# Half of chunk 1's first matrix product by two groups of seven half-size products

## The chip, the core and the metric

One NeuronCore of a Trainium2 chip runs the kernel. Its engines work side by side, each on its own list of instructions, and wait for each other by semaphores: TensorE (PE, with its weight loads shown apart as PEld) multiplies matrices into PSUM, VectorE (DVE) and GpSimd (POOL) do elementwise work, ScalarE (ACT) evaluates functions (Gelu, exp) and copies, and SyncE (SP) issues most transfers. The metric is the device time of one execution in microseconds (us); lower is better.

## The reference

A linear attention, whose result is the input of a two-layer network with an exact Gelu:

```python
# q, k, v: (8 batches, 8 heads, 576 positions, 64)
q_s = softmax(q, axis=-1)          # over the 64 channels
k_s = softmax(k, axis=2)           # over the 576 positions
kv  = einsum('bhsd,bhse->bhde', k_s, v)
x   = einsum('bhsd,bhde->bhse', q_s, kv)
x   = x.transpose(0, 2, 1, 3).reshape(8 * 576, 512)
h   = x @ w_in                     # w_in: 512 x 2048
g   = 0.5 * h * (1 + erf(h / sqrt(2)))
out = g @ w_out                    # w_out: 2048 x 512
```

Inputs and output are float32; the kernel multiplies in bfloat16.

## The kernel before

The 4608 tokens are worked off in nine chunks of 512: chunk c = 0 to 7 holds the first 512 positions of batch c, chunk 8 the last 64 positions of all batches. Every chunk goes through the same stages: exponentials of q and k (ScalarE, `exp_q`, `exp_k`), sums and reciprocals of q (VectorE, `q_sums`) and the multiplication by them (`q_scale`, VectorE or GpSimd), kv = k_s^T v (`kv_mm`, line 231), q transposed (`xbar_step`, a transposing DMA, from batch 2 on), x (`x_mm`), h, Gelu into the tile `g`, and y = g @ w_out (`y_phase`).

The order of the work is written out by hand: an engine carries out its instructions in the order in which the code issues them. Batches run ahead of chunks: while y of chunk c is computed, kv and x of chunk c + 1 and the softmax of batch c + 2 are prepared. `y_phase` takes a dictionary of such insertions, called at numbered points (`after(0)` to `after(10)`).

h of one chunk has 16 tiles of 128 rows. Plainly (chunks 0 and 1), each tile is 4 products of 512 columns (`h_mm`, line 393) and one Gelu (`h_gelu`, line 399). From chunk 2 on `h_waves` computes h by seven half-size products instead of eight (a scheme of the Strassen kind): for each group q of four tiles, 7 products of 4 matmuls with 256 columns each (line 513). Products 1, 2 and 4 take blocks of w_in as they are (`wi_bf`), products 5, 6, 7 and 3 take sums s1 to s4 of blocks (`quad_s`, made once by `quad_weights`: group 0, 1 from `quad_weights(0)`, group 2, 3 from `quad_weights(1)`). Products 4 to 7 multiply sums t1 to t4 of blocks of x (`quad_t`, `x_sums`). The four PSUM results are combined: `seed` copies product 1 (bank A) into bank C, `p5_copy` copies product 5 (bank B) to `r` in SBUF, `e_sum` adds A (after product 6) and r into B, `r_sum` adds A (after product 7) and r into r. Products 7 and 4 accumulate into A and so come after the sums that read it. Gelu is then taken of C, r, A and B.

y too is computed by seven products from chunk 1 on (`y_operands`): its operands are sums of blocks of g (`s5`, `s12`, and differences in place, all by `s_parts`, on VectorE) and mixed blocks of w_out (`mix_wo`: 1 and 6 into `w16`, 7 into `w7`, 3 and 4 in place). From chunk 3 on the product of the quarter blocks in y is itself done by seven products of a smaller size (class `Two`, weights by GpSimd, `y3.weights`).

Around chunk 1, in the order of the code: GpSimd casts three of the four head pairs of v(1) (`cast_v`, line 196); x of chunk 1 comes in two halves with the first tiles of h between; four tiles of h (`t1s`) are finished; VectorE makes the last mixed blocks (lines 1168 to 1171); `h_pairs` computes the other twelve tiles in pairs p = 2 to 7 and, after a pair or two, VectorE makes the sums s5 and s12 and the differences (`s_ops`). ScalarE casts v(2) after the pairs p = 3 to 6. VectorE makes s1, s2 and s3 of `quad_weights(1)` beside it, s4 at the start of `y_phase(1)`. Then come `exp_q(2)` and `exp_k(2)` on ScalarE and the products of y: 4 (into `bd`), 5 (`be`), 1 (`ba`), 2 (again into `bd`), then kv of batch 2, then 3, 6 and 7, x of chunk 2, kv of batch 3 and h of chunk 2. Between product 4 and product 2 the bank `bd` is copied to `f`.

In chunk 2, `h_waves` calls `q_late` in the middle: GpSimd multiplies q(3) as a whole, `xbar_step(3)` transposes it, and GpSimd makes the last three weight sums of `Two`.

Of the kernel before, what the change touches and what calls it, by code (L numbers as in the profile page):

```python
# [16 lines left out]
def kernel(  # L17
# [142 lines left out]

    def exp_q(b, parts=1):

        e = attn_sb.tile([128, J, H, D], BF16, tag="eq")
        st[b]["eq"] = e
# [13 lines left out]
        for i, u in sets:  # L178
            nc.scalar.activation(out=dst[:, i], in_=src[:, u], func=AF.Exp)  # L179
# [98 lines left out]

    def q_scale_parts(b):

        for j in range(J):
            for i in (0, 4):
                e = st[b]["eq"][:, j, i:i + 4, :]
                nc.gpsimd.tensor_tensor(  # L284
                    out=e, in0=e, op=ALU.mult,
                    in1=st[b]["recq"][:, j, i:i + 4].unsqueeze(2).to_broadcast([128, 4, D]),
                )
# [113 lines left out]
    def s_parts(c, p0, n, which):  # L401
# [14 lines left out]
        for i, half in ((3, lo), (4, hi)):  # L416
            if i in which:
                tt(out=s12[:, a, half], in0=g[:, a, half], in1=g[:, b, hi], op=ALU.add)  # L418
        if 2 in which:
            tt(out=g[:, a, hi], in0=g[:, a, hi], in1=g[:, a, lo], op=ALU.subtract)  # L420
            tt(out=g[:, b, lo], in0=g[:, b, lo], in1=g[:, b, hi], op=ALU.subtract)  # L421

# [24 lines left out]

    def quad_weights(w):

# [3 lines left out]
        a21, a22 = wi_bf[:, 0:2, dn], wi_bf[:, 2:4, dn]  # L453
        s1, s2, s3, s4 = (q[:, i] for i in range(4))
        return [
            lambda: tt(s1, a21, a22), lambda: tt(s2, s1, a11, ALU.subtract),
            lambda: tt(s3, a11, a21, ALU.subtract), lambda: tt(s4, a12, s2, ALU.subtract),
        ]
# [19 lines left out]
    def h_waves(c, mid, sums=None):  # L478

        h_begin(c)
        g, xT = st[c]["g"], st[c]["xT"]
# [8 lines left out]
        if mid:  # L492
            bank_of.update(B=("kv0", "kv1") * 2, C=("x1", "x2") * 2)
        held = {}

        def take(kind, q):
            held[kind, q] = bank(roles[bank_of[kind][q]], "q" + kind.lower(), (128, 2, HT))

# [39 lines left out]

        vcopy, scopy = nc.vector.tensor_copy, nc.scalar.copy
        mm(1, 0, 1)  # L540
        seed(0)
        if mid:
# [12 lines left out]
            e_sum(1)  # L555
            mid()
            mm(2, 2, 3)
            gelu("C", 2, 3)
            mm(7, 0, 1)
            r_sum(0)  # L560
            r_sum(1)
            mm(3, 0, 1)
            gelu("B", 0, 1)
# [130 lines left out]
    class Two:  # L694
# [11 lines left out]
        def weights(self, part):  # L706
# [9 lines left out]
            tt(o[2], b21, b11, ALU.subtract, eng=eng)  # L716
            tt(o[3], b11, b12, eng=eng)
            tt(o[4], b21, b22, eng=eng)
            w = self.w[:, 4]
# [58 lines left out]
    def y_phase(c, ins, p3=None):  # L778
# [30 lines left out]
        if p3:  # L809
            p3.mm(c, bx, (4, 5, 1), True)  # L810
            p3.snap(bx)
        mm(4, bd, True)
        if c > 1:
# [8 lines left out]
        else:  # L822
            nc.vector.tensor_copy(out=f, in_=bd)
        after(0)
# [169 lines left out]

    def mix_wo(m, a):

# [11 lines left out]
        }[m]  # L1008
        nc.vector.tensor_tensor(out=o, in0=i0, in1=i1, op=op)

# [89 lines left out]
    w16 = wst.tile([128, 2, HK, HN], BF16, tag="w0", name="w16")  # L1100
    sums = quad_weights(1)
    mix_wo(6, 0)
# [20 lines left out]
    mix_wo(3, 0)  # L1123
    mix_wo(4, 0)
    cast_wo(3, wo[3], 2, 1)
    cast_wo(3, wo[3], 3, 1)
# [155 lines left out]
```

## Time and profile before

| | |
|---|---|
| median of 3 runs | 255.77 us (255.7 to 255.9) |
| the profiled execution | 255.87 us, span 253.9 us |
| mean granted TensorE clock | 0.997 |
| VectorE: two-input bf16 sum, 128x1024 (L409) | 684 ns each, x14 |
| GpSimd: multiplication of q, 128x256 (L284) | 653 ns each, x40 |
| GpSimd: cast of v, 128x576 (L196) | 711 ns each, x25 |
| ScalarE: exponential of k, 128x2304 (L184) | 2120 ns each, x6 |

The span runs from the first instruction to the last; the execution's own time is 1.97 us longer. Durations are means over all instructions of that form. An instruction may begin a little before the one ahead of it has ended, so that start-to-start times in the timeline are often 0.1 us below the durations.

### The profile page before, as it was taken

The numbers are of one execution on the slowest core, as the hardware profiler recorded it, in microseconds if no ns is written. First come the engines' busy times: TensorE is split into PE (matmuls) and PEld (weight loads), VectorE is DVE, ScalarE is ACT, GpSimd is POOL, SyncE is SP. The second block draws the span as 40 slices with busy tenths as digits, with TensorE's granted clock in tenths as the row PEclk, the third lists the DMA queues.
The fourth block names the chain that finished last, engine by engine and source line by source line (L and its number), as shares of the span: only waits on it lengthen the run. The fifth ranks groups of instructions, "written<-read, shape, count | busy, mean of one in ns | idle before, by whom it ended". The sixth has DMA issues, their size and how long they took to land.

```text
span 253.9 us, 6825 instructions
## 1 busy us (share of the span) xinstructions
PE 247.9 (98%) x2738; PEld 196.1 (77%) x2738; DVE 219.1 (86%) x395; ACT 190.4 (75%) x326; POOL 102.8 (40%) x177
## 2 busy tenths in 40 slices
PE   7999999999999999999999999999999999999994
PEld 3444444448888888898889988998889889988883
DVE  1878898788987997998999899989999999868972
ACT  4785978699977996889688968896887788248711
POOL 1530023000978459106950596059603960560000
PEclk9999999999999999999999999999999999999998
DMA  7999999995329999890569255810520061004033
GB/s 239 397 367 420 405 406 400 401 407 206 61 64 288 375 265 377 246 340 5 188 196 310 98 188 177 204 36 3 165 87 3 1 193 57 3 4 165 0 84 84
DMA packets 43168, 50.24 MB, mean 198 GB/s; under 512 B 20225, under 2 KB 30465, under 8 KB 42881
## 3 DMA queue, kind: packets, MB, share of 16 engines
q1 hardware_dynamic: 42416, 49.13, 57.8%
q10 hardware_dynamic: 720, 0.69, 1.0%
q8 instruction: 21, 0.34, 0.6%
q14 instruction: 11, 0.08, 0.1%
HBM read 36.70 MB, written 9.44 MB: 182 GB/s over the span
## 4 chain that ended last, share of the span: by engine, by line
PE 81%; DMA 16%; DVE 1%; SPq 0%; issue 0%
PE qa L513 19%; PE ya L799 10%; PE qb L513 10%; PE yd L799 10%; DMA f<-in_q_dram 7%; PE ye L799 6%; PE ps L393 6%; PE yb L799 5%; PE qc L513 5%; DMA w<-in_moe_w_out_dram 3%; DMA w<-in_moe_w_in_dram 3%; PE yx L753 3%; DMA f<-in_v_dram 2%; PE kv L231 2%; PE ps L359 1%; PE ya L882 1%
## 5 line engine op out<-in xcount | busy, mean ns | idle before, releaser
L513 PEld LDWEIGHTS <-quad_s 128*128 128x128 bf16 x448 | 43.8, 98 | 5.1
L799 PEld LDWEIGHTS <-g 128*128 128x128 bf16 x368 | 35.2, 98 | 4.8 <-issue 0.4
L513 PEld LDWEIGHTS <-wi_bf 128*128 128x128 bf16 x336 | 32.8, 98 | 3.9
L799 PEld LDWEIGHTS <-s 128*128 128x128 bf16 x336 | 32.7, 98 | 3.7
L513 PE MATMUL qa<-quad_t,quad_s 128*128 128x256 bf16 x224 | 29.2, 273 | 0.0
L275 POOL TENSOR_TENSOR e<-e,recq 128x1024 bf16<-128x1024 bf16 (+1 forms) x4 | 9.3, 2330 | 47.8 <-DVE recq L270 41.0
L393 PE MATMUL ps<-xT,wi_bf 128*128 128x512 bf16 x128 | 28.1, 379 | 0.2 <-DVE kvc L244 0.2
L444 POOL TENSOR_TENSOR y_sb<-y_sb 128x128 f32<-128x128 f32 x56 | 26.0, 498 | 2.8 <-issue 2.8
L269 DVE TENSOR_REDUCE qsum<-e 128x16 f32<-128x1024 bf16 (+1 forms) x12 | 20.9, 1746 | 6.8 <-ACT e L179 6.5
L284 POOL TENSOR_TENSOR e<-e,recq 128x256 bf16<-128x256 bf16 x40 | 24.7, 653 | 1.8 <-DVE recq L270 1.2
L393 PEld LDWEIGHTS <-wi_bf 128*128 128x128 bf16 x128 | 12.4, 98 | 15.3 <-issue 0.7
L521 ACT COPY qc<-qa 128x512 f32<-128x512 f32 x26 | 13.9, 577 | 11.4 <-PE qa L513 5.3
L399 ACT ACTIVATE g<-ps 128x512 bf16<-128x512 f32 x32 | 17.6, 602 | 6.1 <-PE ps L393 5.8
L179 ACT ACTIVATE e<-f 128x512 bf16<-128x512 f32 (+1 forms) x42 | 20.5, 556 | 2.1 <-DMA f<-in_q_dram 1.9
L537 ACT ACTIVATE g<-r 128x512 bf16<-128x512 f32 x28 | 17.3, 631 | 6.3 <-DVE r L444 6.3
L444 DVE TENSOR_TENSOR qb<-qa,r 128x512 f32<-128x512 f32 x28 | 18.1, 691 | 4.1 <-PE qa L513 1.6
L537 ACT ACTIVATE g<-qc 128x512 bf16<-128x512 f32 x28 | 15.2, 594 | 7.4 <-PE qc L513 7.4
L418 DVE TENSOR_TENSOR s<-g 128x1024 bf16<-128x1024 bf16 x28 | 19.8, 726 | 0.0
L196 POOL CAST v_aug<-f 128x576 bf16<-128x576 f32 x25 | 17.0, 711 | 4.4 <-DMA f<-in_v_dram 4.3
L444 DVE TENSOR_TENSOR r<-qa,r 128x512 f32<-128x512 f32 x28 | 17.9, 680 | 0.7 <-PE qa L513 0.7
L184 ACT ACTIVATE ek<-f 128x2304 bf16<-128x2304 f32 (+1 forms) x10 | 17.2, 1734 | 1.2 <-DMA f<-in_k_dram 1.2
L1213 POOL CAST scr<-g 128x1 f32<-128x1 bf16 x4 | 0.7, 187 | 42.3 <-DVE g L421 42.3
(117 smaller groups left out, 550.2 us busy)
## 6 DMA issues: line engine op xcount, KB each, us to landing
out_dram<-y_sb SPq DMA_DIRECT2D x16, 512.0 KB, 3.9
f<-in_k_dram SPq DMA_DIRECT2D x6, 1152.0 KB, 9.5
f<-in_v_dram SPq DMA_DIRECT2D x6, 1152.0 KB, 10.5
f<-in_q_dram SPq DMA_DIRECT2D x6, 1024.0 KB, 7.6
w<-in_moe_w_in_dram SPq DMA_DIRECT2D x6, 512.0 KB, 8.9
f<-in_v_dram SPq DMA_DIRECT2D x8, 288.0 KB, 6.5
f<-in_q_dram SPq DMA_DIRECT2D x4, 512.0 KB, 9.0
w<-in_moe_w_out_dram SPq DMA_DIRECT2D x2, 1024.0 KB, 11.4
```

What stands on the lines that cost most here:

```text
L179: nc.scalar.activation(out=dst[:, i], in_=src[:, u], func=AF.Exp)
L184: nc.scalar.activation(out=ek[b % 2][:, i:i + n], in_=st[b]["kf"][:, i:i + n].rearrange("p x (n d) -> p x n d", n=NS), func=AF.Exp,)
L196: eng.tensor_copy(out=o, in_=i)
L269: nc.vector.reduce_sum(out=qsum, in_=st[b]["eq"][:, :, i * w:(i + 1) * w, :], axis=AX.X)
L284: nc.gpsimd.tensor_tensor(out=e, in0=e, op=ALU.mult, in1=st[b]["recq"][:, j, i:i + 4].unsqueeze(2).to_broadcast([128, 4, D]),)
L393: nc.tensor.matmul(ps, wi_bf[:, dm, t * 128:(t + 1) * 128], st[c]["xT"][:, dm, :], start=(dm == 0), stop=(dm == NDM - 1),)
L399: nc.scalar.activation(out=st[c]["g"][:, t, :], in_=ps, func=AF.Gelu)
L418: tt(out=s12[:, a, half], in0=g[:, a, half], in1=g[:, b, hi], op=ALU.add)
L444: eng.tensor_tensor(out=out, in0=in0, in1=in1, op=op)
L513: nc.tensor.matmul(held[kind, q][:, u], w, mov[m][:, k], start=(m in (1, 5) and u == 0 and k == 0), stop=(k == 1), skip_group_check=True,)
L537: nc.scalar.activation(out=g[:, t:t + 2, half], in_=held[kind, q], func=AF.Gelu)
L799: nc.tensor.matmul(ps[:, j * HN:(j + 1) * HN], act[m][:, k, j * 128:(j + 1) * 128], wgt[m][:, k, :], start=(first and k == 0 and j == 0), ...
```

## The change

Of chunk 1's h, the tiles of the second half of each block (groups q = 2, 3; tiles 4 to 7 and 12 to 15) are computed by the seven products; the tiles of p = 0 to 3 stay plain. So `h_waves` gets a branch for chunk 1, with its own banks, and `h_pairs` isn't called any more. `quad_weights(1)` must be ready earlier: s1 is made by VectorE ahead of the last casts of w_out, s2 to s4 by GpSimd in four pieces of 128x256 each, and the mixed blocks 1 and 3 of the second half likewise; they stand behind the casts of v(1) in GpSimd's order, and ahead of all four casts of v(2), which move from ScalarE to GpSimd. VectorE gets the four sums of x of chunk 1, the sums of A and r, and the copies of r.

In `y_phase(1)`, ScalarE makes the copy f of `bd` (VectorE before), between the two halves of `exp_q(2)`; `exp_k(2)` follows. The multiplication of the first half of q(2) is done by GpSimd in four pieces, and the sums and multiplication of q(3) are split in halves, the second half in the middle of chunk 2's h, behind the weight sums of `Two`, which are in pieces of half the size.

```diff
-    def exp_q(b, parts=1):
+    def exp_q(b, parts=1, part=None):
...
-            for h in (0, 4):
+            for h in (0, 4) if part is None else (4 * part,):
...
-    def q_scale_parts(b):
+    def q_scale_parts(b, half=None):
...
-            for i in (0, 4):
+            for i in (0, 4) if half is None else (4 * half,):
...
     def quad_weights(w, parts=()):
...
+        def block(i, out, in0, in1, op=ALU.add):
+            if i not in parts:
+                tt(out, in0, in1, op)
+                return
+            for k in range(2):
+                for n in (slice(0, 256), slice(256, 512)):
+                    tt(out[:, k, n], in0[:, k, n], in1[:, k, n], op, eng=nc.gpsimd)
...
     def h_waves(c, mid, sums=None):
...
+        first_banks = {"A": (5, 6), "B": (1, 7), "C": (3, 4)}
+
+        def plain(p):
+            for i, t in ((2, p + HK), (0, p)):
+                ps = bank(i)
+                h_mm(c, ps, t, range(NDM))
+                h_gelu(c, ps, t)
...
+        if c == 1:
+            plain(2)
+            for q in (2, 3):
+                mm(5, q)
+                mm(1, q)
+            seed(2)
+            seed(3)
+            p5_copy(2, vcopy)
+            p5_copy(3, vcopy)
+            mix_wo(4, 1)
+            plain(3)
+            mm(6, 2, 3)
+            e_sum(2)
+            e_sum(3)
+            mm(2, 2, 3)
+            gelu("C", 2, 3)
+            s_parts(c, 2, 2, (0,))
+            mm(7, 2, 3)
+            r_sum(2)
+            r_sum(3)
+            gelu("r", 2, 3)
+            mm(3, 2, 3)
+            mm(4, 2, 3)
+            gelu("A", 2, 3)
+            gelu("B", 2, 3)
+            s_parts(c, 2, 2, (1,))
+            s_parts(c, 4, 4, (0,))
+            s_parts(c, 4, 4, (3,))
+            s_parts(c, 4, 4, (4,))
+            s_parts(c, 2, 2, (2,))
+            s_parts(c, 4, 4, (5,))
+            return
...
     def y_phase(c, ins, p3=None):
...
+        if c == 1:
+            exp_q(2, parts=2, part=0)
         mm(4, bd, True)
...
-            nc.vector.tensor_copy(out=f, in_=bd)
+            nc.scalar.copy(out=f, in_=bd)
+            exp_q(2, parts=2, part=1)
+            exp_k(2)
...
-    def mix_wo(m, a):
+    def mix_wo(m, a, parts=False):
...
+        if parts:
+            for i in range(4):
+                nc.gpsimd.tensor_tensor(out=o[:, i], in0=i0[:, i], in1=i1[:, i], op=op)
...
-    sums = quad_weights(1)
+    sums = quad_weights(1, parts=(2, 3, 4))
...
     mix_wo(4, 0)
+    sums[0]()
...
-    mix_wo(7, 1)
-    mix_wo(4, 1)
-    mix_wo(1, 1)
-    mix_wo(3, 1)
+    for fn in sums[1:]:
+        fn()
+    for m in (1, 3):
+        mix_wo(m, 1, parts=True)
+    cast_v_all(2)
...
-    h1 = {p + 3: [lambda p=p: cast_v(2, p, nc.scalar)] for p in range(HP)}
-    h1[1] = [sums[0]]
-    h1[3] += sums[1:3]
-    h_pairs(1, h1, done=t1s, turn=Banks(2, 0, 5, 6))
-
-
-    exp_q(2, parts=2)
-    exp_k(2)
+    x_sums(1, (1, 2, 3, 4))
+    mix_wo(7, 1)
+    s_ops(1, 0, 2)
+    h_waves(1, None)
...
     y_phase(1, {
-        0: [sums[3]],
-        7: [lambda: norm_q(2, 0, 2)],
-        1: [lambda: norm_q(2, 1, 2, nc.vector)],
+        7: [lambda: q_sums(2, 0, 2), lambda: q_scale_parts(2, 0)],
+        1: [lambda: norm_q(2, 1, 2, nc.vector), lambda: s_parts(1, 4, 4, (6,))],
...
-        3: [lambda: kv_step(2), lambda: exp_k(3), lambda: q_sums(3)],
+        3: [lambda: kv_step(2), lambda: exp_k(3), lambda: q_sums(3, 0, 2)],
...
-        q_scale(3, nc.gpsimd)
+        q_scale_parts(3, 0)
+
+    def q_later():
+        y3.weights(1)
+        q_sums(3, 1, 2)
+        q_scale_parts(3, 1)
         xbar_step(3)
-        y3.weights(1)
...
-        h_waves(c, q_late if c == 2 else None, p3 and p3.sums)
+        h_waves(c, (q_late, q_later) if c == 2 else None, p3 and p3.sums)
```

(`s_parts` numbers 5 and 6 are the two halves of its number 2. In `h_waves`, `mid[0]` stands where `mid` stood, `mid[1]` after the r sums of groups 0 and 1.)

More of the change, by code (lines that the diff above doesn't have):

```diff
@@ L159, in load_qrest @@
             )
-    def exp_q(b, parts=1):
-        e = attn_sb.tile([128, J, H, D], BF16, tag="eq")
-        st[b]["eq"] = e
+    def exp_q(b, parts=1, part=None):
+        if part != 1:
+            st[b]["eq"] = attn_sb.tile([128, J, H, D], BF16, tag="eq", name="e")
+        e = st[b]["eq"]
         dst = e.rearrange("p j h d -> p h j d")
@@ L277, in q_scale @@
         )
-    def q_scale_parts(b):
+    def q_scale_parts(b, half=None):
+        r = st[b]["recq"]
         for j in range(J):
-            for i in (0, 4):
+            for i in (0, 4) if half is None else (4 * half,):
                 e = st[b]["eq"][:, j, i:i + 4, :]
+                i = i if half is None else 0
                 nc.gpsimd.tensor_tensor(
                     out=e, in0=e, op=ALU.mult,
-                    in1=st[b]["recq"][:, j, i:i + 4].unsqueeze(2).to_broadcast([128, 4, D]),
+                    in1=r[:, j, i:i + 4].unsqueeze(2).to_broadcast([128, 4, D]),
                 )
@@ L418, in s_parts @@
                 tt(out=s12[:, a, half], in0=g[:, a, half], in1=g[:, b, hi], op=ALU.add)
-        if 2 in which:
+        if 2 in which or 5 in which:
             tt(out=g[:, a, hi], in0=g[:, a, hi], in1=g[:, a, lo], op=ALU.subtract)
+        if 2 in which or 6 in which:
             tt(out=g[:, b, lo], in0=g[:, b, lo], in1=g[:, b, hi], op=ALU.subtract)
@@ L446, with quad_weights @@
     quad = {"s": {}}
-    def quad_weights(w):
+    def quad_weights(w, parts=()):
         q = quad["s"][w] = wst.tile([128, 4, 2, 512], BF16, tag=("w4", "w1")[w], name="quad_s")
@@ L478, in h_waves @@
     def h_waves(c, mid, sums=None):
-        h_begin(c)
+        if c > 1:
+            h_begin(c)
         g, xT = st[c]["g"], st[c]["xT"]
@@ L494, in h_waves @@
         held = {}
+        first_banks = {"A": (5, 6), "B": (1, 7), "C": (3, 4)}
[4 more added lines that the diff above has]
+                h_gelu(c, ps, t)
         def take(kind, q):
-            held[kind, q] = bank(roles[bank_of[kind][q]], "q" + kind.lower(), (128, 2, HT))
+            i = first_banks[kind][q - 2] if c == 1 else roles[bank_of[kind][q]]
+            held[kind, q] = bank(i, "q" + kind.lower(), (128, 2, HT))
         def mm(m, *qs):
@@ L555, in h_waves @@
             e_sum(1)
-            mid()
+            mid[0]()
             mm(2, 2, 3)
@@ L561, in h_waves @@
             r_sum(1)
+            mid[1]()
             mm(3, 0, 1)
@@ L715, in weights @@
                 return
-            tt(o[2], b21, b11, ALU.subtract, eng=eng)
-            tt(o[3], b11, b12, eng=eng)
-            tt(o[4], b21, b22, eng=eng)
+            for a in range(2):
+                tt(o[2][:, a], b21[:, a], b11[:, a], ALU.subtract, eng=eng)
+                tt(o[3][:, a], b11[:, a], b12[:, a], eng=eng)
+                tt(o[4][:, a], b21[:, a], b22[:, a], eng=eng)
             w = self.w[:, 4]
@@ L1008, in mix_wo @@
         }[m]
-        nc.vector.tensor_tensor(out=o, in0=i0, in1=i1, op=op)
+        if parts:
+            for i in range(4):
+                nc.gpsimd.tensor_tensor(out=o[:, i], in0=i0[:, i], in1=i1[:, i], op=op)
+        else:
+            nc.vector.tensor_tensor(out=o, in0=i0, in1=i1, op=op)
     def warm(n, z):
```

4 lines of the change are left out of this document (2 added, 2 removed).

## The prediction

> **What bounds the kernel now.** I read the page's busy table first, then the chain of waits, then ScalarE's and VectorE's timelines in chunk 1 (40 to 75 us).
>
> ```profile
> span 253.9 us, 6825 instructions
> PE 247.9 (98%) x2738; PEld 196.1 (77%) x2738; DVE 219.1 (86%) x395; ACT 190.4 (75%) x326; POOL 102.8 (40%) x177
> ```
>
> TensorE (PE) is busy 98% of the span. VectorE (DVE) follows at 86%, so what is laid on it has little room.
>
> ```profile
> 45.48 13.06 PE ps L393 x60
> 58.54 1.75 PE yd L799 x16
> 60.28 1.75 PE ye L799 x16
> 62.03 1.75 PE ya L799 x16
> 63.78 1.75 PE yd L799 x16
> 65.52 0.76 PE kv L231 x72
> ```
>
> The chain (start, duration, what) is TensorE without a hole from 44.12 to 250.34 us. So fewer columns on TensorE shorten the kernel one for one, and any wait put into TensorE lengthens it likewise. One 512-column product of h takes 13.06/60 = 0.218 us; a 256-column one takes 0.109 (1.75/16).
>
> ```profile
> 57.90 1.27 ACT L399 ACTIVATE g<-ps 128x512 bf16<-128x512 f32 x2
> 59.19 1.28 ACT L179 ACT_TABLE_LOAD   x1
> 60.48 2.38 ACT L179 ACTIVATE e<-f 128x512 bf16<-128x512 f32 x6
> 62.76 2.11 ACT L184 ACTIVATE ek<-f 128x2304 bf16<-128x2304 f32 x1
> 64.78 2.17 ACT L179 ACTIVATE e<-f 128x512 bf16<-128x512 f32 x4
> ```
>
> ScalarE's timeline (start, duration) between chunk 1's last Gelu and kv of batch 2: the exponentials of k end at 62.76 + 2.11 = 64.87, and TensorE comes to kv at 65.52. The slack is 0.65 us.
>
> ```profile
> 75.07 0.42 DVE L444 TENSOR_TENSOR quad_t<-xT 128x512 bf16<-128x512 bf16 x1
> ...
> 200.29 0.78 DVE L444 TENSOR_TENSOR quad_t<-xT 128x512 bf16<-128x512 bf16 x1
> 200.75 0.79 POOL L284 TENSOR_TENSOR e<-e,recq 128x256 bf16<-128x256 bf16 x1
> 201.17 0.65 DVE L444 TENSOR_TENSOR quad_t<-xT,quad_t 128x512 bf16<-128x512 bf16 x1
> 201.50 0.79 POOL L284 TENSOR_TENSOR e<-e,recq 128x256 bf16<-128x256 bf16 x1
> ```
>
> The same VectorE operation, first with GpSimd (POOL) idle, then with GpSimd multiplying pieces of 128x256. Alone it takes 0.42 us. Beside the pieces it takes 0.78 and 0.65, and the pieces take 0.79 where a piece with no such neighbour takes 0.61 (start 121.06). The two take turns: the second operation ends at 201.82, 0.42 after 201.40, and 201.40 is 0.14 before the end of the piece begun at 200.75. VectorE's sums that read PSUM beside the same pieces keep their 0.68, so only operations with two SBUF inputs wait.
>
> **The change, part by part.** Times are in the coordinates of the profiled execution.
>
> *TensorE.* The tiles of p = 4 to 7, 32 matmuls of 512 columns, become 2 x 28 of 256: 32 x 0.218 = 6.97 against 56 x 0.109 = 6.12, that is -0.85 us. Without waits, h ends at T = 57.69 instead of 58.54, and kv(2) is reached at T + 4 x 1.746 = 64.67.
>
> *ScalarE.* It loses the four casts of v(2) and gains two seeds (0.58 each) and the copy of yd to f (0.46 of start-to-start time, as 66.86 to 67.32). Its last eight Gelus now hang on VectorE: in chunk 2 the last of them ends 3.90 after the first r sum starts (83.16 to 87.06). That sum could start after product 7's first half, 55.51, and behind VectorE's e sums and one s5 sum, 55.55. So the Gelus end at 59.45 at best. Behind that, in the order of the changed program: table load, half of exp_q, f copy, other half, exp_k, 3.57 (59.19 to 62.76) + 0.48 + 2.11 later. exp_k(2) ends at 65.62, 0.75 later than now, while TensorE arrives 0.85 earlier. So even with nothing else wrong kv(2) starts near 65.65 instead of 65.52: **the saving is eaten by a wait of 0.98, net +0.1**. Queued behind kv on TensorE is all that follows.
>
> *GpSimd's new pieces.* Three block sums are 12 pieces of 128x256, two mixed blocks 8 more, behind the casts of v(1), which end at 42.38. Their own form isn't in the trace; the 512-wide weight sums have 1.11 start to start (81.79 to 82.90), so 0.56 for 256, as L284's 0.57. Without neighbours they run to 53.7 and the casts of v(2) to 56.2 (0.62 each); s4 is needed at 55.9, s2 at 53.3, w16 at 61, v(2) at 65. These edits cost GpSimd nothing on the path; with that cover gone it is the last rival.
>
> *What the pieces do to VectorE.* The added x sums and quadrant sums go on VectorE. From 46.17 it has four x sums, mix 7, the four s operations of p = 0, 1, two r copies from PSUM, mix 4, and then the e sum, which TensorE's product 7 waits for. Start-to-start times in the trace:
>
> ```profile
> 46.17 0.68 DVE L1009 TENSOR_TENSOR w<-wo_bf 128x1024 bf16<-128x1024 bf16 x1
> ...
> 49.39 0.43 DVE L409 TENSOR_TENSOR s<-g 128x512 bf16<-128x512 bf16 x1 [0.61 <-ACT g L399]
> ...
> 84.36 0.93 DVE L418 TENSOR_TENSOR s<-g 128x1024 bf16<-128x1024 bf16 x1
> 87.75 0.68 DVE L409 TENSOR_TENSOR s<-g 128x1024 bf16<-128x1024 bf16 x1
> ```
>
> Alone: 4 x 0.33 + 0.60 brings it to 48.1; the s operations wait for Gelu until 49.39 and take 0.34 + 0.72 + 0.34 + 0.34; copies 1.20; mix 0.60. It would be free at 52.9, before the e sum's input (53.81). But ten of these have two SBUF inputs, and GpSimd's pieces run through all of it. With a turn of 0.42 per operation: t1 starts at 46.22, t2 to t4 and mix 7 at 46.97, 47.72, 48.47, 49.22; the s operations at 50.24, 51.00, 52.14, 52.90; copies 53.24 to 54.44; mix 4 waits to 54.82; the e sums run from 55.42 to 56.62. An s5 sum with a turn against a cast comes between, and the first r sum starts near 57.2 instead of 55.55: **+1.65**. Bounds of a turn: 0 (the sum at 97.62 takes its 0.42, between two pieces) and 0.47 (a piece from 200.18 holds 200.29 back to 200.65). I take 0.42, since back to back each side always finds the other waiting. With 0, the net stays +0.1; with 0.2 it is +0.25 (the gate at 49.39 and the slack before the e sum absorb nearly all).
>
> The Trainium skill speaks against this change: its page "SBUF — State Buffer", section "Who interferes with whom", says that a VectorE operation with two SBUF inputs and a GpSimd one that reads SBUF exclude each other, and that whichever issues second is blocked until the first has finished. The trace agrees on the exclusion (the 0.78 and 0.65 above), but its turns end 0.14 before the piece does; what the rule would make of the time, read strictly, is rival 4.
>
> *Sum at kv(2).* Gelus end at 57.2 + 3.90 = 61.10, exp_k at 67.28, kv starts at 67.3: **+1.8**. TensorE itself, held 0.95 at product 7, is there at 65.9 and waits 1.4. Past it, chunk 1 holds: xbar(2) issues near 68.8 and landing takes 3.7 (median of its issues), before x at 73.4; VectorE takes half of q_sums(3) later and is free at 72.8, before ya ends at 73.4.
>
> *Chunk 2.* q_sums(3)'s second half (1.42) fits VectorE's idle 1.46 before 81.57. GpSimd's multiplication of q(3) is split around the weights: 4 pieces to 79.4, six weight pieces 3.4, the negation 1.5, and then four new pieces from 84.3, where VectorE starts s sums. Four turns less the 0.26 already paid at 84.36 move the s5 sum from 87.75 to 89.2, its end to 89.85. TensorE's ye starts at 88.80 and reaches that half 4 x 0.109 later, at 89.24: **+0.6** (0 without turns, 0.8 at 0.47 each). xbar(3) issues some 7 us later than now, near 87.5 against 80.75; x(3) starts at 95.79, so 3.7 for landing is covered; if not, up to 1 us.
>
> *Sum.* 255.87 (this execution's own time; its span is 253.9, 1.97 lies around it) + 1.8 + 0.6 = 258.3; the median 255.77 is 0.1 lower, so **258.2**.
>
> **Rivals.**
> 1. *The pieces hardly hold VectorE back* (turns up to 0.2). For: the sum at 97.62 slips in free, with pieces on both sides. Against: 123.40, 149.04, 174.64 and 200.29 all wait 0.36 or more. Then only ScalarE's delay is left, +0.1 to +0.25: 255.9 to 256.0, not slower.
> 2. *The saving arrives*: the exponentials of k(2) are ready when TensorE is. Place: kv(2); price -0.85, 254.9. It decides at 64.67, and a wait there under 0.34 would still be over 0.2% faster. For: TensorE is otherwise full, and ScalarE loses 2.6 us of casts. Against: from T on ScalarE needs 1.76 for Gelus and 6.18 behind, against TensorE's 6.98.
> 3. *GpSimd becomes the bound*: if every piece waits for a 1024-wide operation (0.6 + 0.47), 20 pieces and four casts end at 42.3 + 21.4 + 4.9 = 68.6, and kv(2) waits for v instead, +1.3 on the forecast: 259.5. Against: half the turns are 0.33 wide, and PSUM operations leave it alone.
> 4. *A turn costs a whole piece*, 0.57 start to start and not 0.42: ten turns add 1.5 to the forecast, 259.7. For: where a piece is itself held back it takes 0.79. Against: 200.29 is let in at 200.65, 0.14 before the piece's end. This is the page's rule by the letter.
>
> **How the numbers follow.** Forecast 0.72 (its own range 256.8 to 259.4: the first term 1.0 to 2.5, the second 0 to 1.1), rival 1 0.14, rival 2 0.06, rival 3 0.04, rival 4 0.04. The likeliest is 258.2. A measurement of this kernel tells 0.2% (0.5 us) from no change; forecast, rival 3 and rival 4 are slower, 0.80, rival 1 same, rival 2 faster. The range, 256.0 to 259.8, takes in rivals 3 and 4 and the edge of rival 1; rival 2 and most of rival 1 are left out.
>
> **What would show it.** Right: chunk 1's x sums near 0.75 apart and GpSimd's sum pieces near 0.8 each between 46 and 53 us; the first r sum of chunk 1 near 57; TensorE idle near 1 us before product 7 and 1.4 before kv(2), released by ScalarE's ek; a short wait at ye of chunk 2 for s. Wrong: x sums 0.33 to 0.4 apart; no wait of TensorE at kv(2); or the wait there released by v_aug. The forecast falls if the last Gelu of chunk 1 ends before 60 us.

## The result, and the profile after

| | before | after |
|---|---|---|
| median, us (lowest to highest of 4 runs) | 255.74 (255.49 to 255.9) | 258.74 (258.61 to 259.58) |
| ratio, 95% interval | | 1.0125 [1.0102, 1.0149] |
| the profiled execution, us (its span) | 255.87 (253.9) | 259.58 (257.8) |

The kernel is slower by 3.0 us (2.6 to 3.8 by the interval); 2.4 was forecast. The profiled execution of the changed kernel is the longest of its four: the spans of the others are 256.8 to 257.0.

The busy table of the changed kernel, and TensorE's waits from 44 us to the end (what waits, for which result, us in total, times, the longest):

```profile
span 257.8 us, 6918 instructions
PE 247.8 (96%) x2762; PEld 198.4 (77%) x2762; DVE 228.4 (89%) x394; ACT 190.0 (74%) x325; POOL 125.8 (49%) x214
```

```profile
PE qa L534 <- DVE qb L448: 1.5, 1, 1.5
PE kv L232 <- ACT ek L185: 1.2, 1, 1.2
PE ye L854 <- DVE s L412: 0.5, 1, 0.5
```

TensorE's busy time is hardly less (247.8 us against 247.9; the ends of matmuls are modelled there and some records are missing, so the saving doesn't show in this sum), and it has three new waits: product 7 for the sums of A and r, kv of batch 2 for the exponentials of k, product 5 of chunk 2's y for the sums s5. These are the three places that the prediction named. The chain of waits of the changed kernel (start, us, what) now leaves TensorE and runs through VectorE and ScalarE:

```profile
46.51 0.97 DVE quad_t L448
47.56 2.33 DVE quad_t L448 x3
49.89 1.07 DVE w L1072
...
54.47 0.69 DVE r L546 x2
56.19 0.74 DVE qb L448 x2
58.23 0.69 DVE r L448
58.94 1.28 ACT g L558 x3
...
62.13 1.28 ACT L180
66.28 2.02 ACT ek L185
68.35 0.83 PE kv L232 x72
92.24 0.61 DVE s L412
92.90 1.48 PE ye L854 x12
```

VectorE is the chain from the first sum of x to the first r sum, ScalarE from there to kv, and a sum s5 ends up on it once more in chunk 2. What stretches VectorE stands in GpSimd's timeline (start, duration, what):

```profile
47.14 3.28 POOL L448 TENSOR_TENSOR quad_s<-wi_bf,quad_s 128x256 bf16<-128x256 bf16 x4
50.38 3.81 POOL L1070 TENSOR_TENSOR w<-wo_bf 128x256 bf16<-128x256 bf16 x4
54.15 3.27 POOL L1070 TENSOR_TENSOR wo_bf<-wo_bf 128x256 bf16<-128x256 bf16 x4
57.37 2.69 POOL L197 CAST v_aug<-f 128x576 bf16<-128x576 f32 x4
```

Pieces of 128x256 take 0.8 to 0.95 us each here.

Where the 3.9 us of this execution are is read from the starts of the same work in TensorE's timeline (by this view kv(2) starts at 65.45 before; the chain of waits, with which the prediction worked, has 65.52):

| us | h of chunk 1 | y of chunk 1 | kv(2) | x(2) | h of chunk 2 | y of chunk 2 | x(3) | last product of chunk 2's y (`ya`) |
|---|---|---|---|---|---|---|---|---|
| before | 44.12 | 58.37 | 65.45 | 71.56 | 72.81 | 85.14 | 95.72 | 96.96 |
| after | 44.46 | 59.99 | 68.35 | 74.45 | 75.70 | 88.26 | 99.55 | 100.80 |
| difference | +0.34 | +1.62 | +2.90 | +2.89 | +2.89 | +3.12 | +3.83 | +3.84 |

(The last column is what the expectations below call chunk 3's last product: the 16 matmuls into `ya` behind kv(3), product 7 of chunk 2's y.) So +2.90 has come about by kv(2), 0.23 in h of chunk 2, 0.71 in its y, and nothing to speak of behind it.

### The profile page after: what moved, and what is told of

It is laid out like the page before. It is cut to its first block, busy times and chain, and to the rows that moved or that the text cites. A ratio compares the mean times of both kernels' runs of the same rounds, so it can differ in the third digit from the quotient of the medians.

```text
span 257.8 us, 6918 instructions
## 1 busy us (share of the span) xinstructions
PE 247.8 (96%) x2762; PEld 198.4 (77%) x2762; DVE 228.4 (89%) x394; ACT 190.0 (74%) x325; POOL 125.8 (49%) x214
## 3 DMA queue, kind: packets, MB, share of 16 engines
q1 hardware_dynamic: 42416, 49.13, 57.4%
## 4 chain that ended last, share of the span: by engine, by line
PE 76%; DVE 11%; ACT 4%; DMA 4%; issue 2%; POOL 1%; SPq 0%; DVEq 0%; ACTq 0%
PE qa L534 19%; PE qb L534 9%; PE ya L854 9%; PE yd L854 7%; PE ps L396 6%; PE qc L534 5%; PE yb L854 5%; PE ye L854 5%; PE yx L808 3%; DMA f<-in_v_dram 2%; PE kv L232 2%; PE ps L362 2%; DMA f<-in_q_dram 2%; PE ya L941 1%; PE yd L941 1%
## 5 line engine op out<-in xcount | busy, mean ns | idle before, releaser
L534 PEld LDWEIGHTS <-quad_s 128*128 128x128 bf16 x480 | 46.9, 98 | 7.9 <-POOL wo_bf L1070 1.8
L287 POOL TENSOR_TENSOR e<-e,recq 128x256 bf16<-128x256 bf16 x52 | 33.4, 679 | 8.0 <-ACT e L180 6.3
L534 PE MATMUL qa<-quad_t,quad_s 128*128 128x256 bf16 x240 | 31.6, 272 | 1.5 <-DVE qb L448 1.5
L197 POOL CAST v_aug<-f 128x576 bf16<-128x576 f32 x29 | 20.7, 746 | 3.6 <-DMA f<-in_v_dram 3.6
L448 DVE TENSOR_TENSOR qb<-qa,r 128x512 f32<-128x512 f32 x30 | 19.4, 690 | 2.4 <-PE qa L534 1.0
L396 PE MATMUL ps<-xT,wi_bf 128*128 128x512 bf16 x96 | 21.4, 379 | 0.0
L421 DVE TENSOR_TENSOR s<-g 128x1024 bf16<-128x1024 bf16 x30 | 21.2, 729 | 0.0
L448 DVE TENSOR_TENSOR r<-qa,r 128x512 f32<-128x512 f32 x30 | 19.2, 680 | 0.5 <-PE qa L534 0.3
L402 ACT ACTIVATE g<-ps 128x512 bf16<-128x512 f32 x24 | 12.8, 603 | 5.8 <-PE ps L396 5.8
L558 ACT ACTIVATE g<-qb 128x512 bf16<-128x512 f32 x30 | 16.2, 595 | 0.9 <-PE qb L534 0.9
```

The costliest lines, as they stand in the source:

```text
L197: eng.tensor_copy(out=o, in_=i)
L287: nc.gpsimd.tensor_tensor(out=e, in0=e, op=ALU.mult, in1=r[:, j, i:i + 4].unsqueeze(2).to_broadcast([128, 4, D]),)
L396: nc.tensor.matmul(ps, wi_bf[:, dm, t * 128:(t + 1) * 128], st[c]["xT"][:, dm, :], start=(dm == 0), stop=(dm == NDM - 1),)
L448: eng.tensor_tensor(out=out, in0=in0, in1=in1, op=op)
L534: nc.tensor.matmul(held[kind, q][:, u], w, mov[m][:, k], start=(m in (1, 5) and u == 0 and k == 0), stop=(k == 1), skip_group_check=True,)
L558: nc.scalar.activation(out=g[:, t:t + 2, half], in_=held[kind, q], func=AF.Gelu)
```

## The experiments

The theory: VectorE's sums with two SBUF inputs take turns with GpSimd's pieces, which read SBUF too; so the sums of A and r come late, behind them the Gelus, the exponentials of k and kv(2). The rivals: GpSimd's pieces do not matter, and it is the added work, its order or the delay on ScalarE; and, for what remains, other waits. Twelve kernels ran, in five groups; each group's own runs of the kernel before had medians of 255.47 to 255.64.

| | median, us | ratio to before, 95% interval |
|---|---|---|
| e1_writes | 257.1 | 1.0069 [1.0046, 1.0093] |
| e9_writes_long | 257.24 | 1.0054 [1.0037, 1.007] |
| e6_pieces_alone | 260.09 | 1.0169 [1.014, 1.0197] |
| e2_q3_whole | 258.56 | 1.0117 [1.0096, 1.0138] |
| e5_s1_early | 258.53 | 1.012 [1.0094, 1.0146] |
| e3_order | 258.88 | 1.0126 [1.011, 1.0141] |
| e4_kv_late | 258.4 | 1.0104 [1.0087, 1.012] |
| e7_all_three | 257.68 | 1.0087 [1.007, 1.0103] |
| e8_no_reads | 256.66 | 1.0042 [1.0025, 1.0058] |
| e10_half_scaled | 256.54 | 1.0032 [1.002, 1.0043] |
| e11_unscaled | 257.37 | 1.0061 [1.0039, 1.0082] |
| e12_unscaled_held | 256.12 | 1.0018 [1.0009, 1.0028] |

### Is it what GpSimd reads?

**e1_writes.** The twenty pieces write their outputs, but read nothing.

```diff
-                    tt(out[:, k, n], in0[:, k, n], in1[:, k, n], op, eng=nc.gpsimd)
+                    nc.gpsimd.memset(out[:, k, n], 0.0)
...
-                nc.gpsimd.tensor_tensor(out=o[:, i], in0=i0[:, i], in1=i1[:, i], op=op)
+                nc.gpsimd.memset(o[:, i], 0.0)
```

> GpSimd's 20 new pieces (block sums s2 to s4, mixed blocks 1 and 3 of the second half) become memsets of the same outputs: GpSimd is as busy at the same place but reads nothing; the sums themselves are left out. Theory (turns with pieces that read SBUF): VectorE's x sums run 0.33 to 0.4 apart, the first r sum of chunk 1 starts near 56 instead of 58.2, TensorE no longer waits at product 7, kv(2) still waits about 1.0 for the exponentials of k, and the wait at ye of chunk 2 stays; 256.4 us (256.0 to 256.9). Rival (GpSimd's pieces are too slow or stand in the wrong place, or the pieces hold VectorE back whatever they do): 258.3 to 258.7. Rival (ScalarE's longer list alone makes the loss): 258.7.

257.1: 1.6 us of the 3.0 are gone, and the wait at product 7 with them. VectorE's four x sums took 0.41 to 0.43 us. But a memset took 0.27 us and all twenty had ended at 47.1, so GpSimd was idle for most of the time in question: the run cannot tell reading from being busy.

**e9_writes_long.** As e1_writes, with two memsets for each piece of a block sum and three for each of a mixed block.

```diff
-                    tt(out[:, k, n], in0[:, k, n], in1[:, k, n], op, eng=nc.gpsimd)
+                    for _ in range(2):
+                        nc.gpsimd.memset(out[:, k, n], 0.0)
...
-                nc.gpsimd.tensor_tensor(out=o[:, i], in0=i0[:, i], in1=i1[:, i], op=op)
+                for _ in range(3):
+                    nc.gpsimd.memset(o[:, i], 0.0)
```

> The changed kernel with GpSimd's pieces as memsets again, but each written two or three times, so that GpSimd is as busy as with the sums (24 + 24 memsets of 0.27 us, from 41.7 to about 54.6; the casts of v(2) behind them). The sums are left out, so the output isn't the reference's. In e1_writes the memsets ended at 47.1, so the gain there could come from GpSimd being idle afterwards and not from its reading nothing. Theory (only a GpSimd operation that reads SBUF holds VectorE): x sums 0.42 us, mixed block 7 and the s sums unheld to 54.6, then at most one or two turns beside the casts of v(2); first r sum near 55.7 to 56.1, no wait at product 7 over 0.4; 257.1 to 257.4 (range 256.6 to 257.8). Rival (any busy GpSimd holds VectorE): x sums 0.7 to 0.9, r sum near 58, 258.6.

257.24, as expected. Again the sums themselves are left out. GpSimd's timeline in this kernel:

```profile
42.17 7.51 POOL L466 MEMSET quad_s<- 128x256 bf16 x24
49.63 4.02 POOL L1072 MEMSET w<- 128x256 bf16 x12
53.59 4.02 POOL L1072 MEMSET wo_bf<- 128x256 bf16 x12
57.55 3.41 POOL L197 CAST v_aug<-f 128x576 bf16<-128x576 f32 x4
```

and VectorE's beside it:

```profile
46.68 0.43 DVE L448 TENSOR_TENSOR quad_t<-xT,quad_t 128x512 bf16<-128x512 bf16 x1
47.02 0.42 DVE L448 TENSOR_TENSOR quad_t<-xT 128x512 bf16<-128x512 bf16 x1
47.36 0.42 DVE L448 TENSOR_TENSOR quad_t<-xT,quad_t 128x512 bf16<-128x512 bf16 x1
47.69 0.68 DVE L1074 TENSOR_TENSOR w<-wo_bf 128x1024 bf16<-128x1024 bf16 x1
...
55.59 1.29 DVE L448 TENSOR_TENSOR r<-qa,r 128x512 f32<-128x512 f32 x2
...
58.55 0.82 DVE L412 TENSOR_TENSOR s<-g 128x1024 bf16<-128x1024 bf16 x1 [1.07 <-ACT g L559]
59.29 1.15 DVE L421 TENSOR_TENSOR s<-g 128x1024 bf16<-128x1024 bf16 x1
```

GpSimd is busy without a gap until 57.55, as with the sums, and VectorE isn't held: the x sums start 0.34 apart, and the first r sum starts at 55.59, where 55.55 was the prediction's value for no turns. From 57.55 GpSimd reads again (the casts of v(2)), and a sum that takes 0.68 alone takes 0.82 and 1.15. So what holds VectorE is GpSimd's reading of SBUF, and these twenty pieces' reading is worth some 1.5 us of the 3.0. The Trainium skill says just that on its page "SBUF — State Buffer", section "Who interferes with whom": a VectorE operation with two SBUF inputs contends with a GpSimd one that reads SBUF, and not with one that only writes it.

The whole gain lies ahead of kv(2), which starts at 65.72 here (65.45 before, 68.35 in the changed kernel; 65.65 was the prediction's value without turns) and still waits 1.00 for the exponentials of k. So 0.27 of the loss is left at kv(2), the part of ScalarE's longer way. The other 1.4 come in chunk 2, 0.67 in its h and 0.70 in its y, where GpSimd's reading was left as it is. In e8_no_reads, which also has the four moves of e7_all_three, only 0.2 is left there; which of them takes the rest away was not separated.

**e6_pieces_alone.** The kernel before, with twenty such sums by GpSimd into a tile that nobody uses, and nothing else.

```diff
+    for i in range(20):
+        tt(extra, wi_bf[:, 0, 0:256], wi_bf[:, 1, 0:256], eng=nc.gpsimd)
     mix_wo(7, 1)
     mix_wo(4, 1)
```

> The kernel before the change, with 20 sums of 128x256 by GpSimd added behind the casts of v(1); they read w_in and write a scratch tile that nothing uses. Theory: some 14 of them meet VectorE's sums of chunk 1, 0.43 each, 6.0 in all less VectorE's idle 2.1; the s sums of the last pair come 3.9 late, TensorE waits some 2.3 at ye or ya of chunk 1: 258.0 us (257.4 to 258.8). Rival (the loss is in the products' own chain of e and r sums, the pieces alone harm nothing): 255.6 to 255.9.

260.09, +4.5 and 1.3 above the expected range. VectorE is held as expected. The chain of waits runs through VectorE from 45.03 to 63.31:

```profile
45.72 1.09 DVE w L1010
46.83 1.04 DVE wo_bf L1010
...
53.52 1.07 DVE quad_s L445
...
58.11 2.15 DVE quad_s L445 x2
...
63.31 2.10 PE ye L800 x9
```

Each 1024-wide sum takes 1.04 to 1.09 instead of 0.60 from start to start. Fifteen sums pay a turn (some 14 were expected; in the old kernel VectorE makes the sums of weights itself), and TensorE waits 2.4 at ye, where 2.3 was expected.

What the expectation did not have is TensorE's clock. From the start of y to kv(2) TensorE takes 11.57 us instead of 7.08. Some 3.0 of the 4.5 are standing still at ye, from start to start, and 1.5 are slower matmuls behind it: the granted clock is 0.50 from 63.3 to 65.2 us and 0.73 from there to 67.5, the last nine matmuls of ye take 1.89 instead of 0.98 us, and the sixteen of ya 2.36 instead of 1.75. The three runs with a mean clock of 0.992 to 0.993 took 259.89 to 260.59 us, the one with 0.998 took 258.9. In every other trace of this case the granted clock is 1.00 from 44 to 250 us. So by these figures the pieces alone would cost the old kernel some 3.0 without the lower clock, about what the whole change costs.

### The other terms: q(3) in halves, and s1 ahead of the casts

**e2_q3_whole.** The sums and the multiplication of q(3) are made whole, as before; the rest stays.

```diff
-        3: [lambda: kv_step(2), lambda: exp_k(3), lambda: q_sums(3, 0, 2)],
+        3: [lambda: kv_step(2), lambda: exp_k(3), lambda: q_sums(3)],
...
-        q_scale_parts(3, 0)
+        q_scale(3, nc.gpsimd)
+        xbar_step(3)
+        y3.weights(1)
...
-        y3.weights(1)
-        q_sums(3, 1, 2)
-        q_scale_parts(3, 1)
-        xbar_step(3)
```

> Chunk 2 as before the change: sums of q(3) whole, one GpSimd multiplication of the whole q(3), its transposition, then the weight sums (still in half-size pieces). Theory: the four pieces that ran beside VectorE's s sums are gone, so the wait at ye of chunk 2 (0.5 in the trace, some 0.9 with what leads to it) goes: 257.8 us (257.6 to 258.2); VectorE loses up to 0.3 of it in y of chunk 1. Rival (that wait is only what is left of chunk 1's delay, VectorE being behind): 258.5 to 258.8.

258.56, no gain that can be told from none. The wait at chunk 2's ye is gone, as expected, and y of chunk 2 to x(3) takes 10.57 as before, but TensorE waits for VectorE earlier:

```profile
PE qa L534 <- DVE qb L448: 1.1, 1, 1.1
PE kv L232 <- ACT ek L185: 1.0, 1, 1.0
PE qa L534 <- DVE xT L387: 0.7, 1, 0.7
```

The whole sum of q(3) takes VectorE 2.21 us at 71.20, the copies of xT come behind it, and h of chunk 2 waits 0.7 for them. The split of q(3) costs 0.7 at ye and saves as much here.

The run shows something else too. Up to y of chunk 1 its instructions are those of the changed kernel, yet its kv(2) starts at 67.31 and not at 68.35. VectorE's timeline in e2_q3_whole:

```profile
56.85 0.41 DVE L412 TENSOR_TENSOR s<-g 128x512 bf16<-128x512 bf16 x1
57.19 1.28 DVE L448 TENSOR_TENSOR r<-qa,r 128x512 f32<-128x512 f32 x2
```

and in the changed kernel:

```profile
57.39 0.92 DVE L412 TENSOR_TENSOR s<-g 128x512 bf16<-128x512 bf16 x1
58.23 1.28 DVE L448 TENSOR_TENSOR r<-qa,r 128x512 f32<-128x512 f32 x2
```

The s5 sum fell between two of GpSimd's operations in the one execution (0.41) and behind one in the other (0.92). How many turns VectorE pays differs from one execution to the next; in e4_kv_late, too, whose instructions are the same up to y of chunk 1, mixed block 4 and s5 both paid (1.21 and 0.92), and the r sum started at 57.96.

**e5_s1_early.** s1 stands behind mixed block 7, ahead of the sums of q(1), and no longer behind mixed block 4, ahead of the last casts of w_out.

```diff
     mix_wo(7, 0)
+    sums[0]()
...
     mix_wo(4, 0)
-    sums[0]()
```

> s1 alone moves: VectorE makes it behind mixed block 7 of the first half, ahead of the sums of q(1), where GpSimd is idle, and no longer beside GpSimd's casts of v(1). Theory (s1 and the turn it takes with a cast delay kv and x of chunk 1 by 0.35): h of chunk 1 starts near 44.1 as before the change; 258.4 us (258.2 to 258.6). Rival (the later start is only the arrival of v(1) and w_out in that execution): 258.7.

258.53; its interval takes in the changed kernel's ratio, 1.0125, so a gain of 0.2 to 0.3 is neither shown nor excluded. h of chunk 1 started at 44.02, but at 44.28 in e2_q3_whole and 44.00 in e4_kv_late, which have s1 at its place in the changed kernel. The start at 44.46 was largely a matter of that execution. Its r sum started at 57.02, its kv(2) at 67.14.

### Can the waits be moved away?

**e3_order.** VectorE makes the sums that TensorE needs first, and the s sums of p = 0 to 3 and mixed block 7 behind the r sums. Mixed block 7 is made there from blocks that mixed block 4 has already changed.

```diff
-    mix_wo(7, 1)
-    s_ops(1, 0, 2)
     h_waves(1, None)
...
-            s_parts(c, 2, 2, (0,))
             mm(7, 2, 3)
...
             gelu("B", 2, 3)
+            s_parts(c, 0, 2, (0,))
+            s_parts(c, 2, 2, (0,))
+            s_parts(c, 0, 2, (1,))
             s_parts(c, 2, 2, (1,))
...
+            s_parts(c, 0, 2, (2,))
             s_parts(c, 2, 2, (2,))
...
+            mix_wo(7, 1)
```

> VectorE's order alone: mixed block 7 and the s sums of p = 0 to 3 move behind the r sums of chunk 1; GpSimd's pieces stay. Theory: the turns stay 0.4 each, but five of them and 3.8 us of sums no longer stand ahead of the e and r sums; e sums start near 54.3, the first r sum near 56, kv(2) near 66.3; s5 may be late for ye by up to 0.4: 256.9 us (256.5 to 257.4). Rival (the e sums wait for something else, TensorE's product 6 or the copies of r): 258.5 or more.

258.88: a miss of 2 us. The wait at product 7 is gone and the r sum starts at 55.47, but TensorE's longest waits are now these:

```profile
PE ye L858 <- DVE s L412: 1.2, 2, 0.7
PE ya L858 <- DVE y_sb L448: 0.8, 1, 0.8
PE ps L362 <- DVE recq L271: 0.4, 1, 0.4
```

VectorE's work was put off, not made less: the same backlog ends up in y of chunk 1. VectorE, not the order of its work, is short of time between 46 and 72 us.

**e4_kv_late.** kv(2) stands behind product 3 of y instead of ahead of it.

```diff
-        3: [lambda: kv_step(2), lambda: exp_k(3), lambda: q_sums(3, 0, 2)],
-        10: [lambda: table(AF.Gelu)],
+        3: [lambda: exp_k(3), lambda: q_sums(3, 0, 2)],
+        10: [lambda: kv_step(2), lambda: table(AF.Gelu)],
```

> kv of batch 2 moves behind product 3 of y of chunk 1, 1.75 later on TensorE; nothing else. Theory: the exponentials of k(2) are then ready in time (68.30 against about 68.9), the wait of 1.2 goes, the waits at product 7 (1.46) and in chunk 2 stay: 257.5 us (257.2 to 257.9). Rival (the exponentials are not what kv waits for, but v or the bank): 258.7.

258.4: a miss, some 0.3 less than the changed kernel and not 1.2, and the intervals do not tell 0.3 from nothing. The wait for ek is gone, and x(2) waits 0.6 us for `qT`: the exponentials of q(2) hang on the same late Gelus, and behind them come the multiplication and the transfer.

**e7_all_three.** The changes of e4_kv_late and e5_s1_early, the copies of r by ScalarE, and the weight sums of `Two` split around the second half of q(3).

```diff
-            p5_copy(2, vcopy)
-            p5_copy(3, vcopy)
+            p5_copy(2, scopy)
+            p5_copy(3, scopy)
...
-        def weights(self, part):
+        def weights(self, part, half=(0, 1)):
...
-            for a in range(2):
+            for a in half:
...
+            if 1 not in half:
+                return
...
-        y3.weights(1)
+        y3.weights(1, (0,))
...
+        if c == 2:
+            yi[4] = [lambda: y3.weights(1, (1,))]
```

> The changed kernel with four moves together: s1 early; the copies of r in chunk 1 by ScalarE and not by VectorE (1.2); kv(2) behind product 3; of the last weight sums, the first three ahead of the second half of q(3), the rest and the negation at the end of chunk 2. Theory: terms of 0.35, 1.2, 1.2 and 0.9 go, of which x of chunk 2 takes back 0.7 waiting for the transposed q(2): 256.0 us (255.4 to 256.8). Rival (VectorE is full from 46 to 75 us, so that each wait taken away comes back at the next place): 257.5 to 258.2.

257.68, 1.1 us less than the changed kernel and 2.1 more than the one before: a miss of 1.7, within the rival's range. This is the fastest version of the change found that computes everything the reference does. The waits at kv(2) and ye are gone, product 7 waits 0.4 and x(2) 0.8 for `qT`.

### What still keeps the saving back without any turns?

**e8_no_reads.** As e7_all_three, with the pieces as memsets (the sums of weights are left out).

> The same four moves, and GpSimd's 20 pieces as memsets (the sums left out). Theory: without turns and with the exponentials in time TensorE has no wait left in chunks 1 and 2, and the seven products bring what they save: 0.85 under the kernel before, 254.9 us (254.6 to 255.4). Rival (the seven products' own sums on VectorE, or ScalarE's delay, cost more than the products save even so): 255.7 to 256.5.

256.66: a miss of 1.8 us. Nothing in chunk 1's h waits any more: h runs from 43.90 to 57.36, 13.46 us against 14.25 before, so the products do save some 0.8. TensorE has one wait left from 44 us on, that of x(2):

```profile
PE ps L362 <- DMA qT<-e: 1.0, 1, 1.0
```

x(2) starts at 71.58, where it started at 71.56 before. The Gelus end at 59.28; from there the table load, the exponentials of q(2), the sums, the multiplication in two halves and the transfer, issued at 67.09, take 12.3 us.

**e10_half_scaled, e11_unscaled, e12_unscaled_held.** This path is shortened by leaving work out: in e10_half_scaled the multiplication of the second half of q(2), in the other two all of it. In e12_unscaled_held GpSimd waits for `f` before its casts of v(3). The core of the edits:

```diff
-        7: [lambda: q_sums(2, 0, 2), lambda: q_scale_parts(2, 0)],
-        1: [lambda: norm_q(2, 1, 2, nc.vector), lambda: s_parts(1, 4, 4, (6,))],
-        2: [lambda: cast_v_all(3), first_weights, lambda: xbar_step(2), lambda: exp_q(3)],
...
+        7: [lambda: q_sums(2, 0, 2)],
+        1: [lambda: q_sums(2, 1, 2), lambda: s_parts(1, 4, 4, (6,))],
+        2: [lambda: nc.gpsimd.tensor_copy(out=scr[:, 2:3], in_=zeros32[:, 0:1]),
+            lambda: cast_v_all(3), first_weights, lambda: xbar_step(2), lambda: exp_q(3)],
```

(e10_half_scaled has the second of the three lines, e11_unscaled the first two.)

> As e8_no_reads (four moves, GpSimd's pieces as memsets), and VectorE's multiplication of the second half of q(2) is left out, besides the sums of weights, so the output isn't the reference's. It shortens the path exp_q(2), sums, multiplication, transposing DMA, x(2): the transfer then waits for GpSimd's pieces alone (65.85 in e8_no_reads) and is issued near 65.9 instead of 67.09. Theory (that path is what keeps back the saving of the seven products once VectorE isn't held): the wait of x(2) for qT, 1.0 us, goes or falls under 0.2, x starts at 70.6 to 70.8, and the time is 255.7 (255.3 to 256.1). Rival (another wait takes its place, at the casts of xT, kv(3) or ye): the wait of x falls but chunk 3's last product starts no earlier than 97.0, 256.3 to 256.8.

256.54. The transfer was issued at 66.33, earlier as expected, but took 5.5 us to landing instead of 4.4, so x(2) started at 71.93. The wait that was to go grew to 1.3; the run decides nothing.

> As e10_half_scaled, and GpSimd's multiplication of the first half of q(2) is left out too (the sums are still made), so q(2) is transposed as soon as ScalarE's exponentials have ended, near 63.5 us; the output isn't the reference's. In e10_half_scaled the transfer was issued 0.76 earlier than in e8_no_reads and landed no earlier (5.5 us to landing instead of 4.4). Here even 5.5 to 6.5 us end before TensorE comes to x(2) at 70.6. Theory (the transfer of q(2) is the last thing that keeps the products' saving back): no wait at x(2), x starts at 70.6 to 70.7, chunk 3's last product at 96.0 to 96.4 (before: 97.0), time 255.3 to 255.8. Rival (something else then waits in chunk 2, such as the casts of xT, kv(3) or ye): x starts early but chunk 3's last product starts after 96.8, time 256.3 or more.

257.37, slower than e10_half_scaled though it does less. VectorE's timeline in e11_unscaled, and the wait that follows:

```profile
59.02 2.22 DVE L421 TENSOR_TENSOR s<-g 128x1024 bf16<-128x1024 bf16 x2
61.16 0.88 DVE L423 TENSOR_TENSOR g<-g 128x512 bf16<-128x512 bf16 x1
61.97 0.88 DVE L425 TENSOR_TENSOR g<-g 128x512 bf16<-128x512 bf16 x1
```

```profile
PE ye L856 <- DVE zeros L448: 1.8, 1, 1.8
```

With no pieces of q(2) to do, GpSimd began the casts of v(3) at 58.94, beside VectorE's sums, which took turns with them: 1.11 instead of 0.65 each, 0.88 instead of 0.42. So the subtraction into `f` was late, and product 3 waited for it. That is the theory's mechanism once more, brought about by the edit itself.

> As e11_unscaled (nothing of q(2) is multiplied, GpSimd's pieces are memsets, so the output isn't the reference's), but GpSimd's casts of v(3) and weight sums of Two are held until VectorE has subtracted be from f, by a copy of one element that reads f. In e11_unscaled GpSimd, with no pieces of q(2) ahead of them, began these casts at 58.94, beside VectorE's s12 sums, which then took 1.11 us each instead of 0.65; f was 2.2 us later and product 3 waited 1.8 us for it. Theory (turns of VectorE with GpSimd's SBUF reads, and behind them the path of q(2) to x(2), are all that keeps the products' saving back): no wait at product 3, none at x(2), x starts near 70.6, chunk 3's last product at 96.0 to 96.4 (before: 97.0), time 255.2 (254.8 to 255.8). Rival (a further wait in chunk 2 takes its place): chunk 3's last product after 96.8, 256.2 or more.

256.12, still 0.18% (0.09 to 0.28) above the kernel before. The collision is gone, x(2) starts at 70.80 without a wait, 0.76 earlier than before; then h of chunk 2 waits for the copies of x(2):

```profile
72.80 1.91 PE L534 MATMUL qa<-xT,wi_bf 128*128 128x256 bf16 x16 [0.68 <-DVE xT L387]
```

It starts at 72.80, and at 72.81 before: VectorE turns to these copies only when it has read chunk 1's last product (`ya`) at 70.91. The rival was nearer (it had the last product after 96.8 and 256.2 us or more; they were 96.87 and 256.12): behind each wait taken away stood the next, and the saving of 0.8 us was used up at h of chunk 2.

What this kernel still loses comes later. At chunk 2's last product it is 0.09 ahead of the kernel before; from there to x(4) it takes 24.68 us, where the kernel before and the changed kernel take 24.40. e8_no_reads, e10_half_scaled and e11_unscaled take 24.65 to 24.67. In these four the weight sums of `Two` that were moved to the end of chunk 2 run on GpSimd into chunk 3 (in e12_unscaled_held from 102.42 to 106.15), and two of VectorE's sums beside them take 0.84 and 0.69 us instead of 0.41 and 0.28. The kernel before has 0.36 of idle time on VectorE ahead of its next e sum, less than that. In e7_all_three the same weight sums hold only one sum (0.75 instead of 0.28), and nothing is lost (24.40). So this last loss fits the same turns, brought about by the edit; no run tests it. Whether it could be carried past that point wasn't tried, nor was a version found that beats the kernel before.

## Why the prediction was right, and where it was off

*TensorE's saving.* Predicted 0.85; where nothing waits (e8_no_reads), 0.8.

*VectorE's turns, the term of +1.65.* The mechanism was right, and is shown: with pieces that read nothing (e9_writes_long) the r sum starts at 55.59 and the kernel takes 1.5 us less. The price of a turn was too low. VectorE's timeline in e5_s1_early:

```profile
47.50 0.88 DVE L448 TENSOR_TENSOR quad_t<-xT 128x512 bf16<-128x512 bf16 x1
48.31 0.89 DVE L448 TENSOR_TENSOR quad_t<-xT,quad_t 128x512 bf16<-128x512 bf16 x1
49.12 1.15 DVE L1072 TENSOR_TENSOR w<-wo_bf 128x1024 bf16<-128x1024 bf16 x1
```

Back-to-back sums of 128x512 start 0.81 apart, against 0.34 beside memsets: 0.47 a turn, the upper bound that was given, not 0.42. The number of turns was taken as fixed (ten, and s5 besides), but varies: the r sum was forecast at 57.2 and started at 57.02, 57.19, 57.96 and 58.23 in four executions (h of chunk 1 started at 44.02, 44.28, 44.00 and 44.46 in them). In e5_s1_early mixed block 4 and s5 paid nothing (0.68 and 0.41 us). So a turn was dearer and the turns were fewer, the two errors cancel in part, and it is partly luck that 57.2 came out so close. By its own terms the prediction should also have had 57.4: the e sums end at 56.62, and s5 with its turn takes 0.34 + 0.42.

*ScalarE behind it.* Predicted 3.90 from the r sum to the last Gelu's end: 62.12 - 58.23 = 3.89. From there to kv(2) 6.2 were predicted, and it was 6.23.

*kv(2) at 67.3.* 67.14 and 67.31 in e5_s1_early and e2_q3_whole, 68.35 in the profiled execution of the changed kernel, whose x sums also began 0.2 to 0.5 later than in those two. TensorE's waits were predicted as 0.95 and 1.4; they were 1.1 and 1.0 in e2_q3_whole, 1.46 and 1.21 in the changed kernel. (TensorE's own arrival at 65.9 does not follow from 64.67 and 0.95, which make 65.6; kv(2) hangs on ScalarE, so the time does not change by it.)

*Chunk 2, +0.6.* The place and the cause (s5 of chunk 2, beside the four new pieces) were right: y of chunk 2 loses 0.71. Another 0.23 in its h, in pauses too short for the list of waits, wasn't in the sum. With kv(2) as in e2_q3_whole (+1.86), 0.23 and 0.71 make +2.8; the medians differ by 3.0.

*"Past it, chunk 1 holds."* It does in the changed kernel: kv(2) to x(2) takes 6.10 and took 6.11. But the slack behind it is small, as e4_kv_late shows, where x(2) waits for `qT` as soon as kv(2) doesn't wait for ek.

*s1 ahead of the casts of w_out*, not priced in the prediction, could not be told from nothing in the time. h of chunk 1 starts at 43.99 to 44.46 in the six traces of changed kernels that have it there, and at 43.87 to 44.16 in the six that have it earlier.

*The rivals.* The first (turns up to 0.2) is refuted by the 0.81 and 0.34 above; its +0.1 to +0.25 is what kv(2) showed once the turns were gone (+0.27 in e9_writes_long). The second (the saving arrives) asked for the exponentials of k(2) to be ready when TensorE is; e8_no_reads brought that about by putting kv(2) later, and the saving still didn't arrive, so the condition that it named isn't enough. The third (GpSimd late for v(2)) did not occur: the casts of v(2) ended at 60.06. The fourth, the rule of that page of the Trainium skill by the letter, would have a turn cost the whole piece, 0.57, and the turn measured is 0.47, so it lies between the value taken and the rule.

## What to carry to other kernels

Work handed from VectorE to GpSimd is not free because GpSimd is idle: if both read SBUF at that time, a two-input sum of VectorE can pay most of one piece of GpSimd's (here up to 0.47 us of 0.57, and sometimes nothing), so count the turns first, by what each operation reads. In a kernel whose first engine is full, a saving on that engine must find every later result ready earlier too; follow each of them (here sums, Gelus, exponentials, a transfer, copies) before booking it. An order that only puts an engine's work off moves its wait downstream.

## What the runs showed of the hardware that wasn't expected

- That GpSimd's memsets don't hold VectorE's two-input sums (starts 0.34 apart beside 24 of them) was expected by then. Its casts from float32 cost them as much as a piece does: 1.11 instead of 0.65 in e11_unscaled, so 0.46.
- How often VectorE loses a turn differs between executions of the same instructions (r sum at 57.19 and 57.96 in e2_q3_whole and e4_kv_late). The changed kernel's four times spread over 0.97 us and those of e5_s1_early over 1.54, as much as or more than all 52 of the kernel before (255.27 to 256.22); that the turns spread them is not shown.
- The transposing transfer of q(2) took 3.7 to 5.5 us from issue to landing in the fourteen traces, and issued 0.76 earlier it landed no earlier (e8_no_reads, e10_half_scaled).
- TensorE's granted clock fell to 0.50 in one kernel only, e6_pieces_alone, behind three waits at ye within 3.7 us; the waits of the other kernels, up to 1.8 us each, left it at 1.00.
